# A fused attention and MLP kernel: MLP groups of 4, 6, 6, 6, 6, 4 and 4 chunks instead of nine groups of 4

## The chip, the cores and the metric

The kernel runs on one core of one Trainium2 chip. The metric is the device time of one execution in microseconds (us). Three runs of the kernel before took 2340.01, 2342.80 and 2343.21 us; their median, 2342.8 us, is the time before. TensorE is called PE here, its weight loads PEld, VectorE DVE, ScalarE ACT, GpSimd POOL, and SyncE, which issues nearly all transfers, SP.

## The reference

The input x is one sequence of 2048 tokens of width 576. Two branches read it, and a gate mixes them:

```python
x = A_x
g = _sigmoid((x * gate_w).sum(-1, keepdims=True))
a = _A_ref(x, A_wqkv, A_wo)     # 32-head attention, head width 18, softmax over 2048 keys
b = _B_ref(x, B_w1, B_b1, B_w2, B_b2)
return g * a + (1 - g) * b

def _B_ref(x, w1, b1, w2, b2):
    y = _layernorm(x, axis=-1)
    h = _gelu(jnp.einsum("bsd,df->bsf", y, w1) + b1)      # 576 -> 4608, tanh form of GELU
    return jnp.einsum("bsf,fd->bsd", h, w2) + b2          # 4608 -> 576
```

All data are 32-bit floats. Products are made from rounded high parts and their remainders (high x high, high x low, low x high), which is why each weight and activation appears as a pair of tiles.

## The kernel before, in words

**Three stretches.** First come the QKV projection, the layer norm and the gate (the first 250 us or so). Then a loop of 512 steps runs the attention, and the whole MLP is cut into pieces that are put between the attention's matmuls. The output projection begins in the last dozen steps and ends alone after the loop.

**The attention step.** There are 32 units (a pair of heads, half of the queries), and each has 16 steps, one per chunk of 128 keys. A step issues, twice: two score matmuls (line 248, called s2 here), whose results ACT turns into exponentials (line 251), and one round of two score matmuls for a later unit (line 208, called s1), whose maxima DVE takes (line 210). An even step also issues the products of probabilities and values for the last two steps (line 266). The s1 rounds run ahead of s2 and end some 20 steps before the loop does. At the end of a unit's rounds its maxima are transposed on PE (line 225) and written by two small transfers into the next query tile; these go out on ACT's queue instead of SP's where a large load of y was issued in the last 20 slots (lines 229 and 122). Five PSUM banks go round for the scores, and two (`ps_w`) belong to the MLP and later to the output projection.

**The pieces.** `mlp()` (line 319) is a generator that yields after every few matmuls. The loop calls `fill` three times in two steps: at the end of an even step (share 0) and twice in the odd step (shares 1 and 2). Each call takes one piece from the generator. A double step, counted from the start of an odd step to the start of the next odd one, thus holds eight s2 and eight s1 matmuls, one block of line 266 and three MLP pieces. Each engine's instructions stand in the order in which this Python code issues them; nothing is reordered later. A slot is one call of `run_due`; there are eight in a double step, and deferred work (GELU stages, weight splits, stores) is issued at slots or when a running estimate of POOL's queue falls due.

**The MLP.** Tokens go in four blocks of 512, the 4608 hidden units in 36 chunks of 128. `h_pair` (line 428) makes two chunks: 27 slots of two matmuls (line 452, 64 rows each, both halves of the array at once), 54 matmuls in all. DVE and ACT add the bias (lines 472 and 473), and GELU runs on ACT (square, line 505; tanh, line 503) and POOL (line 164), six POOL operations per chunk, ending in a high and a low tile (`hp` pool, 6 buffers of each). `out_pair` (line 510) multiplies one group of chunks into 128 tokens: 2 turns x G chunks x 3 products x 2 halves. The second turn swaps the PSUM banks of the two halves, so `nc.tensor.drain()` (line 521) stands between the turns. Then two DVE operations (line 541) add half of each bank's sum into `acc`. A group needs four `out_pair` calls.

With G = 4 there are nine groups in a block. The order (lines 597 to 611) is: first pair of group i, the four `out_pair` of group i-1, loads or splits of the down weights of group i, second pair of group i. The first pair of a group is called with `last=True` and is cut into six pieces of 8, 10, 10, 8, 10 and 8 matmuls (two double steps); the second is cut into three pieces of 18 (one double step). An `out_pair` is cut after 14 and 30 of its 48 matmuls and takes one double step. In a block's last group the second pair stands between the `out_pair` calls. In the first block every weight is read raw, rounded on ACT (line 368), split on POOL and stored to a scratch in DRAM; later blocks reload the pairs from it (W1 pairs 1152 KB, W2 chunks 576 KB; `wp2` has 4 buffers for W2).

**The end.** At steps 489, 494, 497 and 499 (`PSTEP`) the output projection's generator is advanced by hand: wo is loaded, then the attention output (line 915), then its denominators (line 934), and then five multiplications, roundings and differences on DVE and ACT (lines 978, 981 and 988, for the last chunk 984, 985 and 990) are issued slot by slot. Projection pieces of nine matmuls (line 1052) replace MLP pieces once the MLP generator is empty, all sums are stored (line 548), and the step is past 500. Until then an empty generator gives an empty piece.

Of the kernel before, what the change touches and what calls it, by code (L numbers as in the profile page):

```python
# [24 lines left out]
TB = 512  # L25
NPAIR = H // 2
VW = 52
G = 4
NFC = F // P
NG = NFC // G  # L30
ND = 288
SCALE = DH ** -0.5
GC1 = 0.7978845608028654 * 0.044715
# [7 lines left out]
LAND = 8  # L41
GAP = 1130.0
BUSY = 20
TOTAL = NB * NG * (G // 2 * 27 * 231 + 8 * 3 * G * 131)
PLAN = [[(), (0,), (1,), (2,), (3,), (4,), (5, 6), ()], [(), (), (0,), (1,), (2,), (3,), (4,), (5, 6)],
        [(0,), (1,), (2,), (3,), (4,), (5,), (6,), ()]]
LAST = 28
PSTEP = (489, 494, 497, 499)
ORDER = (0, 1, 3, 2)
ROUNDS = [lambda g: 0, lambda g: 0, lambda g: int(g >= 4), lambda g: 1 if g < 9 else 2]  # L50
SKIP = 0
N_AT = 5
# [6 lines left out]
def gated_mix_kernel(ctx: ExitStack, tc: tile.TileContext, x, wqkv, wo, w1, b1, w2, b2, gate_w, out):  # L59
# [24 lines left out]
    b2b = const.tile([P, D], F32, name="b2b")  # L84


    att = ctx.enter_context(tc.tile_pool(name="att", bufs=1))
    yp = ctx.enter_context(tc.tile_pool(name="yp", bufs=2))
    xp = ctx.enter_context(tc.tile_pool(name="xp", bufs=2))
    pp = ctx.enter_context(tc.tile_pool(name="pp", bufs=2))  # L90
    hp = ctx.enter_context(tc.tile_pool(name="hp", bufs=6))
    asm = ctx.enter_context(tc.tile_pool(name="asm", bufs=2))
    ps_s1 = ctx.enter_context(tc.tile_pool(name="ps_s1", bufs=NS1, space=PSUM))
    ps_o = ctx.enter_context(tc.tile_pool(name="ps_o", bufs=1, space=PSUM))
# [19 lines left out]
    def x_tile():  # L114
        return xp.tile([P, 4 * 640], F32, name="x")
# [203 lines left out]
    def mlp():  # L319
# [1 line left out]
        RAW = {}  # L321
        seq = [(tb, g) for tb in range(NB) for g in range(NG)]
        n = len(seq)
        npair = n * (G // 2)
        Y, ACC = {}, {}

        def chunk(q):

            i, m = divmod(q, G // 2)
            return i, m, seq[i][1] * G + 2 * m  # L330


        raws = x_tile()
# [67 lines left out]
                split(W1, q, wp1, shape, (1, q), R1, w1_scr[q], lambda q: load_w1(q + 1))  # L401

        def prep_w2(i):
            for m in range(G // 2):
                q = i * (G // 2) + m
                for j in range(2):
                    c = 2 * (q % NQ0) + j
                    if q >= NQ0:
                        reload(W2, (q, j), wp2, [P, 2, D], w2_scr[c])
                        continue  # L410
                    split(W2, (q, j), wp2, [P, 2, D], (2, c), R2[c % 2], w2_scr[c],
                          lambda c: load_w2(c + 2))
# [97 lines left out]
        def out_pair(i, t, acc):  # L510

            tb, g = seq[i]
            tok = slice(t * P, (t + 1) * P)
            cs = [slice(nn * ND, (nn + 1) * ND) for nn in range(2)]
            ps = [psum(ps_w) for _ in range(2)]
            ends = {7, 15} if piece[0] == 0 else cuts(24, (3, 2, 1)[piece[0]])
            k = 0
            for turn in range(2):
                if turn == 1:

                    nc.tensor.drain()
                for j in ORDER:
# [4 lines left out]
                    w_ = ready(W2, (i * (G // 2) + j // 2, j % 2))  # L527
                    for h_, p_ in ((hh, 0), (hh, 1), (hl, 0)):
                        for h in (0, 1) if turn == 0 else (1, 0):
                            r = slice(64 * h, 64 * h + 64)  # L530
                            nn = h ^ turn
                            nc.tensor.matmul(ps[nn][:, :ND], h_[r, tok], w_[p_][r, cs[nn]],  # L532
                                             start=(k == 0), stop=(k == 6 * G - 1))
                        k += 1
                        if k < 6 * G:
                            if k in ends:
                                cut[0] = 1
                            yield 131
            for nn in range(2):
                dst = acc[:, t, cs[nn]]  # L540
                nc.vector.scalar_tensor_tensor(dst, ps[nn][:, :ND], 0.5, b2b[:, cs[nn]] if g == 0 else dst,  # L541
                                               op0=ALU.mult, op1=ALU.add)
# [18 lines left out]
        def outs(i, between=()):  # L561

            tb, g = seq[i]
            if g == 0:
                ACC[tb] = x_tile().rearrange("p (t d) -> p t d", t=4)[:, :, :D]
# [4 lines left out]
            for j in range(G):  # L570
                HT.pop((i, j))
                W2.pop((i * (G // 2) + j // 2, j % 2))

        load_w1(0)
        for c in range(2):
# [10 lines left out]
        def pair(q, ahead, last=False, inner=False):  # L586
            prep(q + ahead)
            yield from h_pair(q, last, inner)
            i, m, _ = chunk(q)
            if m == 1 and seq[i][1] == NG - 1:  # L590
# [4 lines left out]


        for i in range(n + 1):
            q = 2 * i
            inside = i < n and seq[i][1] == NG - 1
            held = 1 if 0 < i < n and seq[i][1] == 0 else 2  # L600
            if i < n:
                yield from pair(q, held, last=i > 0)
                prep(q + 1 + held)
                if i == n - 1:
                    borrow_w2(q)
            if i > 0:
                yield from outs(i - 1, pair(q + 1, 2, inner=True) if inside else ())
            if 0 < i < n - 1:
                prep_w2(i)
            if i < n and not inside:  # L610
                yield from pair(q + 1, held)

    stream = [mlp()]
    spent = [0.0]
# [33 lines left out]
    with ExitStack() as a:  # L648
# [172 lines left out]
        for tb in range(NB):  # L821
            work = [(qk_group, (tb, mt)) for mt in (range(9) if tb < 2 else (4, 0, 1, 2, 3, 5, 6, 7, 8))] + [(v_group, (tb, t, n)) for t in range(4) for n in range(2)]
            for g, (fn, args) in enumerate(work):
                if tb == 0:
                    if g in W_AT:
                        n = W_AT[g]
                        split_w(n, nc.gpsimd if n > 1 else nc.vector)
                        if n + 2 < 6:
                            load_w(n + 2)
                    if g == 10:  # L830
                        nc.sync.dma_start(b2b, bcast_rows(b2, D))
                        nc.sync.dma_start(b1r, b1.rearrange("(c p) -> c p", p=P))
                if tb == NB - 1 and g == 16:
                    args += (lambda: next(stream[0]),)
                fn(*args)
                ng = g - (N_AT if tb == 0 else 2)
                if 0 <= ng < 4:
                    norm(tb, ng)
                if tb + 1 < NB and 2 <= g < 7:
                    x_chunk(tb + 1, g - 2)  # L840
                yg = g - (11 if tb == 0 else 8)
                if 0 <= yg < 5:
                    y_chunk(tb, yg)
                if g == (16 if tb == 0 else 13) and tb + 2 < NB:
# [311 lines left out]
```

## Time and profile before

| | before |
|---|---|
| median of three runs | 2342.8 us |
| the profiled execution, its own time | 2341.28 us |
| its span in the trace | 2339.5 us |
| PE busy | 2297.5 us (98%) |
| DVE busy | 1655.2 us (71%) |
| ACT busy | 1424.9 us (61%) |
| POOL busy | 966.3 us (41%) |
| mean granted PE clock | 0.994 |

The span is the stretch from the first to the last instruction; the time of an execution is 1.8 us longer. A row of grouped instructions gives line, engine, operation, tiles, shapes, count, then busy time, mean ns of one, then idle time before them and what ended it. A row of the timeline gives start, duration, engine, line and, in brackets, the idle time before it with its releaser. A row of a table by stretches gives the stretch's bounds and length, the busy time of each engine with its instruction count, then the granted clock, the share of the transfer engines and GB/s. Matmuls are pipelined: their durations overlap, so the distance from one start to the next is the better measure of what one costs.

### The profile page before, as it was taken

How to read it: one execution, taken by the hardware profiler on the slowest of the kernel's cores; microseconds unless marked ns; L12 is line 12 of the kernel's file. 1: busy time of each engine (PE TensorE's matmuls, PEld its weight loads, DVE VectorE, ACT ScalarE, POOL GpSimd, SP SyncE). 2: the span in 40 equal slices, each digit the busy share in tenths (PEclk: the TensorE clock that was granted, in tenths of full speed). 3: DMA queues.
4: the chain of work that ended last, by engine and by line, in shares of the span. 5: the costliest groups of instructions: out<-in, count | busy, mean ns of one | idle time of the engine just before them, and what ended most of it. 6: DMA issues, size and time to landing. Idle time of an engine off the chain costs nothing.

```text
span 2339.5 us, 51512 instructions
## 1 busy us (share of the span) xinstructions
PE 2297.5 (98%) x20585; PEld 1571.1 (67%) x20585; DVE 1655.2 (71%) x2890; ACT 1424.9 (61%) x2628; POOL 966.3 (41%) x964
## 2 busy tenths in 40 slices
PE   8999999999999999999999999999999999999999
PEld 7876666666666666666666666666666666666668
DVE  5466677777777777777777777777777777777734
ACT  4222467777676666666666666666666666666662
POOL 3001366666664433333352444444434333333700
PEclk9999899999999999999999999999999999999999
DMA  7648754545456423243263524242364233242264
GB/s 233 237 177 231 198 184 128 169 130 153 136 188 166 158 95 118 93 120 122 82 167 135 163 95 118 95 138 96 118 160 151 95 103 105 101 146 88 80 212 160
DMA packets 164010, 330.31 MB, mean 141 GB/s; under 512 B 57034, under 2 KB 83694, under 8 KB 153042
## 3 DMA queue, kind: packets, MB, share of 16 engines
q1 hardware_dynamic: 162150, 323.76, 44.2%
q8 instruction: 162, 2.65, 0.5%
q10 hardware_dynamic: 1620, 3.26, 0.4%
q14 instruction: 78, 0.64, 0.1%
HBM read 234.16 MB, written 96.58 MB: 141 GB/s over the span
## 4 chain that ended last, share of the span: by engine, by line
PE 94%; DVE 3%; issue 1%; DMA 1%; ACT 1%; SPq 0%; ACTq 0%; DVEq 0%
PE ps L532 21%; PE ps L266 20%; PE ps L452 19%; PE ps L248 13%; PE ps L208 11%; PE ps L769 4%; PE ps L1052 3%; PE ps L790 2%; DVE m L210 1%; PE ps L696 1%; DMA vt<-v_scr 1%; DVE p L756 0%; PE ps L772 0%; PE ps L771 0%; DMA p<-in_A_wqkv_dram 0%
## 5 line engine op out<-in xcount | busy, mean ns | idle before, releaser
L210 DVE TENSOR_REDUCE m<-ps 128x1 f32<-128x512 f32 x2048 | 1316.5, 685 | 465.0 <-PE ps L208 448.1
L251 ACT ACTIVATE p<-ps 128x512 f32<-128x512 f32 x1368 | 742.4, 596 | 408.7 <-PE ps L248 399.3
L164 POOL TENSOR_SCALAR zz<-zz 128x512 f32<-128x512 f32 x288 | 178.4, 620 | 832.0 <-ACT zz L505 816.6
L452 PE MATMUL ps<-big,w 64*128 64x512 f32 x3888 | 513.3, 393 | 0.1
L532 PE MATMUL ps<-w,hh 64*128 64x288 f32 x4352 | 490.7, 299 | 12.2 <-ACT z L473 0.4
L251 ACT ACTIVATE ring<-ps 128x512 f32<-128x512 f32 x680 | 369.3, 596 | 204.8 <-PE ps L248 200.5
L208 PE MATMUL ps<-ka,qa 54*128 54x512 f32 x2048 | 456.0, 415 | 12.1 <-DVE m L210 5.0
L248 PE MATMUL ps<-qa,ka 56*128 56x512 f32 x2048 | 453.8, 423 | 1.2 <-ACT p L251 1.0
L452 PEld LDWEIGHTS ps<-big,w 64*128 64x128 f32 x3888 | 380.7, 185 | 75.3 <-ACT z L473 0.4
L532 PEld LDWEIGHTS ps<-w,hh 64*128 64x128 f32 x4352 | 383.5, 186 | 68.6 <-issue 45.1
L164 POOL TENSOR_TENSOR zz<-zz,z 128x512 f32<-128x512 f32 x288 | 371.7, 1291 | 24.0
L248 PEld LDWEIGHTS ps<-qa,ka 56*128 56x128 f32 x2048 | 205.2, 184 | 214.8 <-DVE m L210 178.8
L266 PE MATMUL ps<-p,vt 128*32 128x512 f32 x2736 | 344.8, 598 | 1.2 <-DMA vt<-v_scr 1.2
L532 PE MATMUL ps<-w,hl 64*128 64x288 f32 x2176 | 334.5, 292 | 0.0
L208 PEld LDWEIGHTS ps<-ka,qa 54*128 54x128 f32 x2048 | 213.7, 187 | 84.4 <-ACT p L251 25.3
L164 POOL TENSOR_TENSOR w<-x,w 128x576 fp32r<-128x576 f32 (+1 forms) x54 | 98.5, 1838 | 307.6 <-DMA qk_scr<-hl 169.0
L532 PEld LDWEIGHTS ps<-w,hl 64*128 64x128 f32 x2176 | 218.1, 185 | 4.9
L164 POOL TENSOR_TENSOR hl<-zz,hh 128x512 fp32r<-128x512 f32 x136 | 176.6, 1298 | 11.4
L266 PEld LDWEIGHTS ps<-p,vt 128*32 128x32 f32 x2736 | 71.6, 109 | 160.8 <-issue 151.8
L266 PE MATMUL ps<-ring,vt 128*32 128x512 f32 x1360 | 179.1, 598 | 0.0
L769 PE MATMUL ps<-big,wqk 128*128 128x512 f32 x432 | 110.6, 405 | 2.9 <-ACT wqk L690 2.0
L541 DVE SCALAR_TENSOR_TENSOR x<-ps,x 128x288 f32<-128x288 f32 x256 | 104.1, 448 | 12.7 <-PE ps L532 12.7
(100 smaller groups left out, 1375.3 us busy)
## 6 DMA issues: line engine op xcount, KB each, us to landing
w<-w_scr SPq DMA_DIRECT2D x54, 1152.0 KB
w<-w_scr SPq DMA_DIRECT2D x108, 576.0 KB
x<-in_B_w_dram SPq DMA_DIRECT2D x72, 288.0 KB
w_scr<-w SPq DMA_DIRECT2D x18, 1152.0 KB
w_scr<-w SPq DMA_DIRECT2D x36, 576.0 KB
big<-y_scr SPq DMA_DIRECT2D x42, 384.0 KB
qa<-qk_scr SPq DMA_DIRECT2D x192, 72.0 KB
ka<-qk_scr SPq DMA_DIRECT2D x84, 144.0 KB
```

The source lines that it names most:

```text
L164: fn(*args, **kw)
L208: nc.tensor.matmul(ps, qa[r0:r0 + 54, t * P:(t + 1) * P], ka[r0:r0 + 54, kb * TB:(kb + 1) * TB], start=True, stop=True)
L210: nc.vector.tensor_reduce(M4[u][:, h, t, kb:kb + 1], ps, axis=AX.X, op=ALU.max)
L248: nc.tensor.matmul(ps[h], ka[r0:r0 + 56, kc * P:(kc + 1) * P], qa[r0:r0 + 56, qb * TB:(qb + 1) * TB], start=True, stop=True)
L251: nc.scalar.activation(RING[n % 3][:, qb, h], ps[h], AF.Exp, scale=SCALE)
L266: nc.tensor.matmul(OB[u][r:r + 32, :], v[:, k, 19 * h:19 * h + 32], RING[c % 3][:, qb, h, :], start=(k == 0), stop=(k == NT - 1))
L452: nc.tensor.matmul(ps[h], wt[w_][r, c, :], Y[s_][r, c, :], start=(k == 0), stop=(k == 26))
L532: nc.tensor.matmul(ps[nn][:, :ND], h_[r, tok], w_[p_][r, cs[nn]], start=(k == 0), stop=(k == 6 * G - 1))
L541: nc.vector.scalar_tensor_tensor(dst, ps[nn][:, :ND], 0.5, b2b[:, cs[nn]] if g == 0 else dst, op0=ALU.mult, op1=ALU.add)
L769: nc.tensor.matmul(ps, w_[:, c, ms], big[:, s_, :], start=(k == 0), stop=False)
L790: nc.tensor.matmul(ps[:, :ND], big[:, s_, tok], w_[:, c, cs], start=(k == 0), stop=False)
L1052: nc.tensor.matmul(ps[:, :ND], OT[b][2][:, s_, tok], w_part(w_, c)[:, cs], start=(k == 0), stop=(k == 13))
```

## The change

The groups of a block become 4, 6, 6, 6, 6, 4 and 4 chunks. There are 28 groups instead of 36, and 112 `out_pair` calls instead of 144, with as many matmuls as before. For the larger groups `hp` has 8 buffers of each kind, and `wp2` has 6. An `out_pair` of six chunks has 72 matmuls, cut into three pieces of 24, with the drain in the middle of the second. All pairs of a group after the first are issued one behind the other, and every pair but those between the `out_pair` calls and the first two is called with `last=True`, so that it takes six pieces (one pair, which the code finds late, five). The bias b2 is no longer held in a tile and added at the first sum: `begin_sums` loads it, broadcast, into `acc` by four transfers of 288 KB on SP per block, one up pair ahead of the block's first sum. The order of the chunks in a sum is 0 to n-3, then n-1, n-2 (for four chunks the same as before). The space for the tiles comes from a smaller reserve (`dynamic_dma_scratch_size`). In the instruction order of the changed program the last MLP matmul stands in step 495 instead of 499; the `PSTEP` numbers and the step from which the projection may begin are the same.

```diff
-G = 4
 NFC = F // P
-NG = NFC // G
+SIZES = (4, 6, 6, 6, 6, 4, 4)
+NG = len(SIZES)
...
-TOTAL = NB * NG * (G // 2 * 27 * 231 + 8 * 3 * G * 131)
+TOTAL = NB * (NFC // 2 * 27 * 231 + 8 * 3 * NFC * 131)
...
-ORDER = (0, 1, 3, 2)
...
-    hp = ctx.enter_context(tc.tile_pool(name="hp", bufs=6))
+    hp = ctx.enter_context(tc.tile_pool(name="hp", bufs=8))
...
+        size = [SIZES[g] for _, g in seq]
+        npair = NB * NFC // 2
...
+        place = [(i, m) for i in range(n) for m in range(size[i] // 2)]
+        first_pair = [place.index((i, 0)) for i in range(n)]
...
         def prep_w2(i):
-            for m in range(G // 2):
-                q = i * (G // 2) + m
+            for m in range(size[i] // 2):
+                q = first_pair[i] + m
...
-            ends = {7, 15} if piece[0] == 0 else cuts(24, (3, 2, 1)[piece[0]])
+            half = 3 * size[i]
+            ends = {7, 15} if piece[0] == 0 and half == 12 else cuts(2 * half, (3, 2, 1)[piece[0]])
+            order = [*range(size[i] - 2), size[i] - 1, size[i] - 2]
...
-                nc.vector.scalar_tensor_tensor(dst, ps[nn][:, :ND], 0.5, b2b[:, cs[nn]] if g == 0 else dst,
+                nc.vector.scalar_tensor_tensor(dst, ps[nn][:, :ND], 0.5, dst,
                                                op0=ALU.mult, op1=ALU.add)
...
+        def begin_sums(tb):
+
+            ACC[tb] = x_tile().rearrange("p (t d) -> p t d", t=4)[:, :, :D]
+            for t in range(4):
+                nc.sync.dma_start(ACC[tb][:, t], bcast_rows(b2, D))
...
         for i in range(n + 1):
-            q = 2 * i
+            q = first_pair[i] if i < n else npair
             inside = i < n and seq[i][1] == NG - 1
             held = 1 if 0 < i < n and seq[i][1] == 0 else 2
+            if i > 0 and seq[i - 1][1] == 0:
+                begin_sums(seq[i - 1][0])
...
             if i < n and not inside:
-                yield from pair(q + 1, held)
+                for m in range(1, size[i] // 2):
+                    yield from pair(q + m, held, last=i > 0)
...
-                        nc.sync.dma_start(b2b, bcast_rows(b2, D))
                         nc.sync.dma_start(b1r, b1.rearrange("(c p) -> c p", p=P))
...
-                        wp2 = mstack.enter_context(tc.tile_pool(name="m_w2", bufs=4))
+                        wp2 = mstack.enter_context(tc.tile_pool(name="m_w2", bufs=6))
...
-    nc = _bacc.Bacc("TRN2", target_bir_lowering=False, num_devices=1)
+    nc = _bacc.Bacc("TRN2", target_bir_lowering=False, num_devices=1, dynamic_dma_scratch_size=1024)
```

More of the change, by code (lines that the diff above doesn't have):

```diff
@@ L83, in gated_mix_kernel @@
     b1t = const.tile([P, NFC], F32, name="b1t")
-    b2b = const.tile([P, D], F32, name="b2b")
     att = ctx.enter_context(tc.tile_pool(name="att", bufs=1))
@@ L323, in mlp @@
         n = len(seq)
-        npair = n * (G // 2)
+        size = [SIZES[g] for _, g in seq]
+        npair = NB * NFC // 2
         Y, ACC = {}, {}
+        place = [(i, m) for i in range(n) for m in range(size[i] // 2)]
+        first_pair = [place.index((i, 0)) for i in range(n)]
         def chunk(q):
-            i, m = divmod(q, G // 2)
-            return i, m, seq[i][1] * G + 2 * m
+            i, m = place[q]
+            return i, m, 2 * (q % (NFC // 2))
         raws = x_tile()
@@ L521, in out_pair @@
                     nc.tensor.drain()
-                for j in ORDER:
+                for j in order:
                     while (i, j) not in HT:
@@ L526, in out_pair @@
                     hh, hl = HT[i, j]
-                    w_ = ready(W2, (i * (G // 2) + j // 2, j % 2))
+                    w_ = ready(W2, (first_pair[i] + j // 2, j % 2))
                     for h_, p_ in ((hh, 0), (hh, 1), (hl, 0)):
@@ L532, in out_pair @@
                             nc.tensor.matmul(ps[nn][:, :ND], h_[r, tok], w_[p_][r, cs[nn]],
-                                             start=(k == 0), stop=(k == 6 * G - 1))
+                                             start=(k == 0), stop=(k == 2 * half - 1))
                         k += 1
-                        if k < 6 * G:
+                        if k < 2 * half:
                             if k in ends:
@@ L563, in outs @@
             tb, g = seq[i]
-            if g == 0:
-                ACC[tb] = x_tile().rearrange("p (t d) -> p t d", t=4)[:, :, :D]
             for t in range(4):
@@ L569, in outs @@
                 yield from out_pair(i, t, ACC[tb])
-            for j in range(G):
+            for j in range(size[i]):
                 HT.pop((i, j))
-                W2.pop((i * (G // 2) + j // 2, j % 2))
+                W2.pop((first_pair[i] + j // 2, j % 2))
+        def begin_sums(tb):
+            ACC[tb] = x_tile().rearrange("p (t d) -> p t d", t=4)[:, :, :D]
+            for t in range(4):
+                nc.sync.dma_start(ACC[tb][:, t], bcast_rows(b2, D))
         load_w1(0)
@@ L589, in pair @@
             i, m, _ = chunk(q)
-            if m == 1 and seq[i][1] == NG - 1:
+            if m == size[i] // 2 - 1 and seq[i][1] == NG - 1:
                 hidden[0] = seq[i][0]
```

## The prediction

> **What bounds the kernel now.** I read the page first, then the chain of waits, then the loop by double steps.
>
> ```profile
> span 2339.5 us, 51512 instructions
> PE 2297.5 (98%) x20585; PEld 1571.1 (67%) x20585; DVE 1655.2 (71%) x2890; ACT 1424.9 (61%) x2628; POOL 966.3 (41%) x964
> PE 94%; DVE 3%; issue 1%; DMA 1%; ACT 1%; SPq 0%; ACTq 0%; DVEq 0%
> PE ps L532 21%; PE ps L266 20%; PE ps L452 19%; PE ps L248 13%; PE ps L208 11%; PE ps L769 4%; PE ps L1052 3%; PE ps L790 2%; DVE m L210 1%; PE ps L696 1%; DMA vt<-v_scr 1%; DVE p L756 0%; PE ps L772 0%; PE ps L771 0%; DMA p<-in_A_wqkv_dram 0%
> ```
>
> The chain of work that ended last is PE for 94%. A busy share alone would not show that PE is full, since matmuls overlap; starts do. The timeline prices one piece of 18 up matmuls and one `out_pair` around its drain:
>
> ```profile
> 999.08 2.26 PE L452 MATMUL ps<-big,w 64*128 64x512 f32 x18
> 1001.17 0.40 PE L248 MATMUL ps<-qa,ka 56*128 56x512 f32 x2
> ```
> ```profile
> 1135.46 0.30 PE L532 MATMUL ps<-w,hh 64*128 64x288 f32 x2
> 1135.59 0.30 PE L532 MATMUL ps<-w,hl 64*128 64x288 f32 x2
> 1135.73 0.42 PE L532 MATMUL ps<-w,hh 64*128 64x288 f32 x4
> 1135.99 0.30 PE L532 MATMUL ps<-w,hl 64*128 64x288 f32 x2
> 1136.37 0.53 PE L532 MATMUL ps<-w,hh 64*128 64x288 f32 x4
> 1136.74 0.30 PE L532 MATMUL ps<-w,hl 64*128 64x288 f32 x2
> 1136.87 0.41 PE L248 MATMUL ps<-qa,ka 56*128 56x512 f32 x2
> ```
> ```profile
> PEld ps L532 <- issue: 45.1, 144, 0.5
> ```
>
> An up matmul costs (1001.17 - 999.08)/18 = 0.116 us, a pair of down matmuls 0.13 us. From 1135.99 to 1136.37, over the drain, it is 0.38 instead of 0.13, and the next two pairs take 0.37 instead of 0.26: a drain costs 0.36 us. The waits show 144 such holes of 45.1/144 = 0.31 us on the weight side; I take 0.35. Now double steps, in a table by stretches:
>
> ```profile
> 340.58:348.60 8.02, 8.00 (x63) 4.58 (x60) 5.16 (x9) 6.31 (x13) 7.68 (x8) 1.00 0.37 99
> 676.91:684.91 8.00, 7.99 (x62) 4.63 (x60) 5.16 (x9) 6.30 (x13) 7.66 (x8) 1.00 0.91 339
> 740.97:748.51 7.54, 7.54 (x66) 4.56 (x64) 5.75 (x10) 6.93 (x14) 4.39 (x4) 1.00 0.62 236
> 781.57:790.61 9.04, 9.04 (x78) 6.07 (x76) 5.25 (x9) 5.82 (x11) 1.30 (x2) 1.00 0.87 299
> 790.61:797.84 7.23, 7.23 (x62) 4.40 (x60) 5.17 (x9) 5.39 (x11) 6.80 (x8) 1.00 0.49 146
> 797.84:804.93 7.09, 7.09 (x67) 4.39 (x64) 5.89 (x11) 5.96 (x12) 4.69 (x6) 1.00 0.89 154
> 804.93:812.44 7.51, 7.43 (x84) 5.08 (x82) 5.79 (x11) 5.37 (x11) 7.00 (x9) 1.00 1.01 392
> ```
>
> By the order of the matmuls, the fourth row has 44 up matmuls, the fifth 28, the sixth 18 up and 14 down, the seventh 48 down and a drain. Taking off 44 x 0.116 and 28 x 0.116 leaves 3.94 and 3.98 for the attention part; I use 3.94. Then the seventh row, 3.94 + 24 x 0.133 + 0.35 = 7.48, holds 0.03 us of waiting, the fifth 0.03, the sixth (3.94 + 2.09 + 0.93 = 6.96) 0.13. PE has next to no idle time to give away here: a removed drain is a gain, and anything that makes PE wait is a loss.
>
> **The change part by part.**
>
> *Drains.* 112 instead of 144: -32 x 0.35 = -11.2 us (bounds 0.31 and 0.38: -9.9 to -12.2). All other matmuls of PE remain.
>
> *Evictions and b2.*
>
> ```profile
> L541 DVE SCALAR_TENSOR_TENSOR x<-ps,x 128x288 f32<-128x288 f32 x256 | 104.1, 448 | 12.7 <-PE ps L532 12.7
> ```
>
> DVE loses 64 x 0.448 = 28.7 us, but waits for PE in each double step (5.79 of 7.51 busy): nothing on the path. The b2 loads add 15 transfers of 288 KB to SP's queue, four at a time, one up pair (14 us, fifth and sixth row) ahead of their use; the seventh row moved 392 GB/s, so 1.2 MB are 3 us. Six W2 reloads (3.5 MB, 9 us at that rate) stand at least two up pairs ahead of use. SP waits there for the last matmul of `outs`, as before; the query and key loads behind it are for a later unit. Both 0. Without that cover DVE's sums would wait first, then `ps_w`, then PE.
>
> *Up pairs over two double steps, blocks 1 to 3.* A pair in one double step waits for nothing (fourth row: what is left there is the base of 3.94), one in two costs 0.03 + 0.13 = 0.16 us: GELU then shares ACT and DVE with scores that come faster. 51 pairs instead of 27 are so cut: +3.8. Of down double steps there are 84 instead of 108, and the longer pieces give ACT and DVE more time: I take off 2 of the 108 x 0.03 = 3.2 that they held. Together +1.8 (0 to +4).
>
> *The same in block 0.* Here ACT also rounds weights.
>
> ```profile
> L251 ACT ACTIVATE p<-ps 128x512 f32<-128x512 f32 x1368 | 742.4, 596 | 408.7 <-PE ps L248 399.3 <-PE ps L208 2.6 <-PE ps L532 0.9
> L505 ACT ACTIVATE zz<-z 128x512 f32<-128x512 f32 x144 | 83.5, 639 | 1.4 <-DVE z L472 1.2
> L368 ACT ACTIVATE w<-x 128x576 fp32r<-128x576 f32 (+1 forms) x54 | 43.6, 845 | 2.3 <-DMA x<-in_B_w_dram 2.2
> ```
>
> Eight exponentials are 4.8 us; two tanh or squares and two rounded W2 chunks bring ACT to some 7.3 us in a double step of 28 up matmuls that PE could do in 7.2. That is the first row (8.02, so 0.8 of waiting); seven such stand in block 0, the second row is the last. By the instruction order each of the four groups of six has three crowded double steps: two W2 roundings beside bias and squares (the third row of the table: 7.54 against 6.97, 0.57), two beside the tanh (0.8), one W1 rounding beside bias and squares (7.9 us of ACT in 7.64, 0.3). 4 x 1.7 = 6.8, plus two of 0.57 in the groups of four, against 7 x 0.8 = 5.6 and one 0.57: +1.8, and I add 1 for a unit's end that now falls into a short double step. +2.8. The low bound is 0; at the high one each of a group's six double steps of up pairs waits 0.8 like the first row: 4 x 4.8 + 1.1 - 6.2 + 1 = +15.
>
> *Rows on ACT's queue.* Two units' rows instead of one follow a load of y within 20 slots.
>
> ```profile
> 1710.89 1.91 ACTq L122 DMA_DIRECT2D qa<-mr  x2
> 1712.85 1.08 ACT L251 ACTIVATE p<-ps 128x512 f32<-128x512 f32 x2 [1.98 <-PE ps L248]
> 1713.49 0.99 PE L208 MATMUL ps<-ka,qa 54*128 54x512 f32 x2 [1.07 <-ACT p L251]
> ```
> ```profile
> 1712.14:1715.55 3.41, 2.26 (x18) 1.45 (x18) 1.61 (x3) 2.58 (x5) 2.07 (x4) 1.00 1.06 220
> 1715.55:1718.96 3.41, 3.41 (x30) 3.25 (x28) 1.29 (x2) 1.60 (x3) 3.16 (x4) 0.50 0.84 172
> ```
>
> ACT stood 1.91 us for two issues, PE waited about 1.7, and then the granted clock was 0.50 for 3.41 us, another 1.7. In the changed order the y loads stand over 10 us ahead of the rows, so I take 1.1 us for each and a half clock in one case of three: 2 x (1.1 + 0.6) - 3.4 = 0 (-1 to +3.4).
>
> *The end.* The MLP is done four steps earlier, and the projection starts no earlier.
>
> ```profile
> 2228.93:2235.47 6.54, 6.46 (x77) 4.42 (x74) 1.51 (x3) 4.34 (x9) 0.74 (x1) 1.00 0.06 21
> 2235.47:2241.99 6.52, 6.44 (x76) 4.39 (x74) 1.08 (x3) 4.34 (x9) 0.74 (x1) 1.00 0.65 207
> 2241.99:2247.87 5.88, 5.80 (x63) 3.70 (x59) 4.30 (x8) 5.08 (x10) 0.00 (x0) 1.00 0.55 176
> ```
> ```profile
> 2237.92 0.39 SPq L934 DMA_DIRECT2D ka<-ot_scr  x1
> 2243.57 1.90 DVE L978 TENSOR_TENSOR x<-x,ka 128x512 f32<-128x512 f32 x3 [4.00 <-DMA ka<-ot_scr]
> 2244.30 1.24 ACT L981 ACTIVATE big<-x 128x512 fp32r<-128x512 f32 x2 [0.73 <-DVE x L978]
> 2263.58 0.69 DVE L978 TENSOR_TENSOR x<-x,den 128x512 f32<-128x512 f32 x1 [5.94 <-DMA den<-ot_scr]
> 2265.52 0.50 PE L248 MATMUL ps<-qa,ka 56*128 56x512 f32 x1 [1.02 <-ACT p L251]
> ```
>
> These are the double steps of steps 495, 497 and 499, 18.94 us. Without 48 + 48 of their down matmuls and two drains PE would need 18.94 - 7.1 = 11.8. But the denominators, issued 2.45 us into step 497 and landed 5.65 us later, hold DVE, ACT's roundings behind it and the exponentials behind those. After: 497 begins at 5.6 (the 5.88 row less its wait), the issue at 7.6 (one store less ahead of it), landing at 13.3; from there DVE's first operation (0.7), three roundings (1.24 for two, so 1.9) and four exponentials (2.1) stand before the banks of step 501's scores are free: 18.0. So 18.0 against 11.8 is +6.2; the next denominators (last rows) are no longer behind late stores and PE's wait of 1.02 there goes: -1. +5.2 (+2.5, with ACT alone as the limit, 8 x 0.55 per double step, to +8).
>
> Sum against the profiled execution, 2341.28: -11.2 + 1.8 + 2.8 + 0 + 5.2 = -1.4, so 2339.9. The median of the runs is 1.5 us above that execution: 2341.4.
>
> **The rivals.** (1) The saving arrives nearly whole. For it: a wait in block 0 needs ACT's crowding to add up, and in the first row ACT is busy for only 6.31 of 8.02; if it adds nothing and the end costs 2.5, the sum is -11.2 + 1.8 + 2.5 = -6.9: 2335.9.
>
> (2) On the other side: ACT falls behind in block 0 and stays behind. Three pairs follow each other, in the first row POOL is busy for 7.68 of 8.02 us, and a tanh that waits for POOL holds all exponentials behind it. At the high bound, +15 instead of +2.8, the sum is +10.8: 2353.6. It decides (0.2% slower than the median) from 1.7 + 6.1/4 = 3.2 us of waiting per group of six. Against it: the same engines have the whole down part of a group to catch up.
>
> (3) The half clock. In the row above it followed a stretch in which PE idled for about a third of 3.41 us; the empty steps leave PE without work for some 6 us in all. Two half-clock windows, 1.7 each, and one more after ACT's queue: +5.1, so 2346.5. The Trainium skill, "TensorE: Matmul & The Clock Gate", Part 1, says that the clock halves after an idle window of about 3.4 us and returns after a busy one. The trace does not agree with the first half: PE worked for 2.26 of the 3.41 us ahead of the drop. By the page's rule the end would cost at most one such window, 1.7.
>
> (4) The drains cost nothing, because DVE and ACT catch up in them. Then all that is left is +9.8: 2352. The seventh row speaks against it: its length is the sum of its parts.
>
> **How the numbers follow.** A measurement of this kernel can tell about 0.2% (4.7 us, so 2338.1 to 2347.5) from no change. The forecast, no change, has 0.41; (1) has 0.27 and is faster; (2) 0.19, (3) 0.08, (4) 0.05. (2) and (4) are slower; (3) lies near the edge and is shared, 0.04 and 0.04. So faster 0.27, same 0.45, slower 0.28. The forecast's own range is 2338 to 2347. The range for 8 in 10 goes from 2334 (rival 1 with the drain at its upper bound and less than 0.16 per up pair) to 2350 (rival 2 at 3.8 us per group of six); the rest of (2), (4) and a tail below are left out.
>
> **What would show it.** 112 holes before line 535 with the same mean; double steps of 72 down matmuls and a drain of 3.94 + 4.79 + 0.35 = 9.1 us; block 0 (steps 13 to 121) with about 3 us more waiting; a double step of steps 497 and 499 that is not 3.0 us but 4 to 7, with DVE waiting for `ka`. I am wrong if a wait appears that no row above has: sums waiting for b2, or scores waiting for the rows behind six W2 loads.

## The result and the profile after

The changed kernel takes 2355.5 us (median of four runs, 2354.04 to 2356.19), the kernel before 2341.9 beside it: a ratio of 1.0057, 95% interval 1.0041 to 1.0073. It is slower by 0.57% and lies above the predicted range of 2334 to 2350. The profiled execution took 2356.05 us.

The page of the changed kernel: its span, the busy times, and the chain of work that ended last, by engine and by line.

```profile
span 2354.3 us, 51380 instructions
...
PE 2300.6 (98%) x20585; PEld 1565.5 (66%) x20585; DVE 1635.6 (69%) x2826; ACT 1423.6 (60%) x2628; POOL 965.1 (41%) x964
...
PE 87%; POOL 4%; DVE 3%; issue 2%; DMA 2%; ACT 1%; SPq 1%; ACTq 0%; POOLq 0%; DVEq 0%
```

PE still reads as 98% busy. The chain tells that the waits have changed: PE's share fell from 94% to 87%, and POOL, which was not in it, has 4%. These shares are no price: 4% of the span would be 94 us, and a kernel below (`both_moved`) has POOL at 5% and takes 17 us less. Two groups of ACT's instructions show new waits, one of them for POOL. Each row ends with ACT's idle time ahead of the group and what ended it; first the kernel before (tanh, weight rounding), then the changed one.

```profile
L503 ACT ACTIVATE zz<-zz 128x512 f32<-128x512 f32 x144 | 91.3, 634 | 0.0
L368 ACT ACTIVATE w<-x 128x576 fp32r<-128x576 f32 (+1 forms) x54 | 43.6, 845 | 2.3 <-DMA x<-in_B_w_dram 2.2
```
```profile
L504 ACT ACTIVATE zz<-zz 128x512 f32<-128x512 f32 x144 | 91.2, 633 | 12.9 <-POOL zz L162 12.9
L369 ACT ACTIVATE w<-x 128x576 fp32r<-128x576 f32 (+1 forms) x54 | 43.8, 844 | 12.2 <-DMA x<-in_B_w_dram 12.0
```

ACT now waits 12.9 us for POOL ahead of the tanh and 12 us for raw weight loads ahead of roundings, with exponentials queued behind both. To see what PE pays, I take each double step's length and subtract its parts: as in the prediction 3.94 for the attention (3.0 once the s1 rounds are over), 0.0667 per down matmul and 0.35 per drain; 0.1165 per up matmul, where the prediction had 0.116; and, read from starts in the same traces, 0.133 per projection matmul and 0.24 for a transpose of maxima. What is left I call its waiting.

| steps | waiting before, us | after | difference | predicted |
|---|---|---|---|---|
| 13 to 122 (block 0) | 11.9 | 29.6 | +17.7 | +2.8 |
| 123 to 490 | 18.7 | 18.4 | -0.3 | +1.8 and 0 |
| 491 to 500 | 0.3 | 10.1 | +9.8 | the end, |
| 501 to 510 | 7.9 | 6.2 | -1.7 | +5.2 in all |
| 32 drains x 0.35 | | | -11.2 | -11.2 |

The sum is +14.3 of the 14.8 us by which the spans of the two profiled executions differ. A table of the changed kernel by stretches (bounds, length, busy time of PE, PEld, DVE, ACT, POOL with counts, granted clock, share of the transfer engines, GB/s) shows the double steps that matter:

```profile
345.82:353.82 8.00, 7.97 (x63) 4.58 (x60) 5.31 (x10) 6.30 (x13) 7.34 (x8) 1.00 0.66 225
376.26:386.32 10.06, 9.88 (x108) 6.98 (x106) 5.98 (x10) 5.61 (x11) 9.47 (x10) 1.00 0.57 177
672.00:689.29 17.29, 10.12 (x61) 5.00 (x58) 5.82 (x10) 7.16 (x14) 6.50 (x6) 0.70 0.95 257
1482.84:1491.91 9.07, 8.99 (x109) 6.72 (x106) 6.52 (x11) 4.34 (x8) 0.00 (x0) 1.00 0.01 2
2247.89:2252.56 4.67, 4.39 (x26) 1.65 (x24) 0.83 (x2) 4.03 (x8) 0.00 (x0) 1.00 0.33 96
2252.56:2263.96 11.40, 6.80 (x28) 1.90 (x24) 5.36 (x9) 6.70 (x14) 0.00 (x0) 0.90 0.63 201
```

The fourth row is a double step of 72 down matmuls in a later block, 9.07 us as predicted; the second is one in block 0, 10.06. The third is step 99: 17.29 us for work of 6.97. The last two are the double steps 497 and 499, which hold no MLP matmul. Here is step 99, on SP's queue, ACT and PE:

```profile
665.94 2.06 SPq L120 DMA_DIRECT2D qa<-qk_scr  x6
668.05 2.12 SPq L120 DMA_DIRECT2D ka<-qk_scr  x6
670.27 0.39 SPq L192 DMA_DIRECT2D vt<-v_scr  x1
670.75 7.61 SPq L354 DMA_DIRECT2D x<-in_B_w_dram  x2
```
```profile
672.50 1.09 ACT L249 ACTIVATE p<-ps 128x512 f32<-128x512 f32 x2 [0.32 <-PE ps L246]
680.31 0.68 ACT L369 ACTIVATE w<-x 128x576 fp32r<-128x576 f32 x1 [6.72 <-DMA x<-in_B_w_dram]
...
682.09 1.06 ACT L249 ACTIVATE p<-ps 128x512 f32<-128x512 f32 x2
```
```profile
675.15 0.40 PE L246 MATMUL ps<-qa,ka 56*128 56x512 f32 x1
682.72 0.79 PE L246 MATMUL ps<-qa,ka 56*128 56x512 f32 x1 [7.17 <-ACT p L249]
```

In the second step of every other unit SP issues the queries, keys and values of a coming pair of heads. Behind them a raw load of two W2 chunks needs 7.61 us to go out; this I call a meeting of loads. ACT's rounding of these chunks is already in its queue and waits 6.72 us; the exponentials behind it keep the PSUM banks of the scores; PE stands for 7.17 us and then needs 0.79 us for what took 0.40. The granted clock is 0.50 from 677.9 to 688.1 us; PE works for 5.4 us of that, which costs it about 2.7 us more. Of block 0's 17.7 us, this one meeting is 10.

### The profile page after: what moved, and what is told of

It reads as the page before. It is cut to its first block, busy times and chain, and to the rows that moved or that the text cites. A ratio compares the mean times of both kernels' runs of the same rounds, so it can differ in the third digit from the quotient of the medians.

```text
span 2354.3 us, 51380 instructions
## 1 busy us (share of the span) xinstructions
PE 2300.6 (98%) x20585; PEld 1565.5 (66%) x20585; DVE 1635.6 (69%) x2826; ACT 1423.6 (60%) x2628; POOL 965.1 (41%) x964
## 4 chain that ended last, share of the span: by engine, by line
PE 87%; POOL 4%; DVE 3%; issue 2%; DMA 2%; ACT 1%; SPq 1%; ACTq 0%; POOLq 0%; DVEq 0%
PE ps L535 20%; PE ps L264 19%; PE ps L453 17%; PE ps L246 12%; PE ps L206 10%; PE ps L779 4%; PE ps L1061 3%; POOL zz L162 2%; PE ps L800 2%; DVE m L208 1%; POOL w L162 1%; DMA x<-in_B_w_dram 1%; POOL hl L162 1%; DMA vt<-v_scr 1%; PE ps L706 1%
## 5 line engine op out<-in xcount | busy, mean ns | idle before, releaser
L453 PE MATMUL ps<-big,w 64*128 64x512 f32 x3888 | 528.4, 393 | 0.9 <-ACT z L474 0.8
L535 PE MATMUL ps<-w,hh 64*128 64x288 f32 x4352 | 467.2, 297 | 9.5
L246 PE MATMUL ps<-qa,ka 56*128 56x512 f32 x2048 | 458.7, 424 | 11.5 <-ACT p L249 10.2
L535 PEld LDWEIGHTS ps<-w,hh 64*128 64x128 f32 x4352 | 376.6, 185 | 57.5 <-issue 35.3
L162 POOL TENSOR_TENSOR hl<-zz,hh 128x512 fp32r<-128x512 f32 x136 | 176.7, 1300 | 11.4
L544 DVE SCALAR_TENSOR_TENSOR x<-ps,x 128x288 f32<-128x288 f32 x224 | 91.6, 450 | 26.8 <-PE ps L535 26.8
```

Of the source, the lines that this page charges most:

```text
L162: fn(*args, **kw)
L246: nc.tensor.matmul(ps[h], ka[r0:r0 + 56, kc * P:(kc + 1) * P], qa[r0:r0 + 56, qb * TB:(qb + 1) * TB], start=True, stop=True)
L453: nc.tensor.matmul(ps[h], wt[w_][r, c, :], Y[s_][r, c, :], start=(k == 0), stop=(k == 26))
L544: nc.vector.scalar_tensor_tensor(dst, ps[nn][:, :ND], 0.5, dst, op0=ALU.mult, op1=ALU.add)
```

## The experiments

Ratios are to the kernel before on the same chip (2340.7 to 2340.9 us), where the changed kernel, which was not run again beside them, would be at about 2354 by its ratio.

**The price of a drain.** `drain_twice`:

```diff
                 for j in order:
+                    if turn == 1 and j == order[size[i] // 2]: nc.tensor.drain()
```

> The changed kernel with one more drain in the middle of the second turn of each out_pair, 112 in all. If a drain costs PE what the rows gave (0.35 us): +39 us, 2395. If DVE and ACT catch up in drains and they cost nothing (rival 4): 0 to +5, up to 2360.

2389.2 us, ratio 1.0207 (1.0188 to 1.0226): 35 us more than the changed kernel, 0.31 us for each of the 112 (0.26 to 0.37 by the two intervals). The waits show the holes on the weight side doubled, first the changed kernel, then `drain_twice`:

```profile
PEld ps L535 <- issue: 35.3, 112, 0.5
```
```profile
PEld ps L536 <- issue: 70.7, 224, 0.5
```

The 0.31 us are a net price. The 29 double steps of 72 down matmuls in blocks 1 to 3 that have no transpose went from a median of 9.07 to 9.42 us, 0.35 for the drain; in return the waiting of steps 13 to 122 is 3.3 us less than in the changed kernel, and that of steps 491 to 500 2.7 us less. So a drain costs PE time, and rival 4 is out.

**Block 0 alone undone.** `block0_fours`:

```diff
+BLOCKS = ((4,) * 9, SIZES, SIZES, SIZES)
-                    yield from pair(q + m, held, last=i > 0)
+                    yield from pair(q + m, held, last=seq[i][0] > 0)
```

> The changed kernel with nine groups of four in the first block, their second pairs in one double step as before, and 4, 6, 6, 6, 6, 4, 4 in the other three; the last MLP matmul stays in step 495. Theory Q+C: all that block 0 lost (waiting of 29.6 us against 11.9) is the larger groups' doing, so -17.7, and 8 drains more, +2.8: 2340.6 us. If only the meeting of the value load with a raw W2 load mattered and the groups of four meet it too, only the crowding goes: -7.6 + 2.8, 2350.7. If block 0 has nothing to do with it, +2.8: 2358.

2343.5 us, ratio 1.0013 (1.0004 to 1.0021). Block 0's waiting is 12.2 us, step 99's 0.2. Nearly the whole loss of block 0 belongs to the larger groups there. The run does not tell the meeting of loads from crowding, that is, from more work on ACT and POOL than a double step has room for.

**The meeting of loads.** `v_parts` cuts the value load into four:

```diff
...
-                    load_v(u // 2 + 1)
+            if kc in (1, 3, 5, 7) and u % 2 == 0 and u // 2 + 1 < NPAIR: load_v(u // 2 + 1, 2 * kc - 2, 2 * kc + 2)
```

> The changed kernel with the value load of the next pair of heads (416 KB in rows of 208 bytes, one transfer) cut into four of 104 KB, two steps apart. Theory Q (queue): in step 99 a raw load of W2 stood 7.61 us in SP's queue behind that load, ACT's rounding of it waited 6.72 us with all exponentials behind, PE stood 7.17 us, and then ran at half clock (10.3 us in all); steps 39 and 43 lost 3.9 us by the same meeting at step 33. Then 10 to 13 us go: 2342.5 to 2345.5 us. Theory C (crowding): three up pairs in a row in block 0 keep ACT and POOL late, whatever the loads do; then at most 2 us go: 2353.5 to 2356. In both the end (steps 497 to 501, 16.1 us) stays.

2351.8 us, ratio 1.0049 (1.0037 to 1.0062), about 2 us gained and not 10. Step 39 lost its 2.0 us, step 99 went from 10.3 to 8.4 only. The rows of this run say why:

```profile
668.80 0.39 SPq L192 DMA_DIRECT2D vt<-v_scr  x1
669.28 1.37 SPq L354 DMA_DIRECT2D x<-in_B_w_dram  x2
...
677.04 1.40 ACT L369 ACTIVATE w<-x 128x576 fp32r<-128x576 f32 x2 [5.30 <-DMA x<-in_B_w_dram]
```

The raw load now goes out in 1.37 us, but lands 6 to 8 us later, behind the queries and keys: the value load is not the whole obstacle. `loads_late` moves all three loads three double steps later in block 0:

```diff
-            if kc == 1:
+            if kc == (7 if u < 8 else 1):
                 if u + 2 < NU:
                     load_q(u + 2)
```

> The changed kernel with the query, key and value loads of the next pair of heads three double steps later in the first block (at the eighth step of a unit instead of the second), so that the raw loads of W2 in steps 33 to 38 and 97 to 101 have no such loads ahead of them. The run with the value load in four parts took only 2 us of the 10.3 out of step 99: there the raw W2 load went out 1.5 us sooner, but it still stood behind 0.9 MB of query and key loads and landed 7.7 us later. Theory Q2 (it is all of the loads at a pair's change, in issue and in bytes, that make the raw load late): the whole of step 99's stall and the 2.0 us of step 39 go, -11 to -13: 2341.5 to 2343.5 us where the changed kernel would be at 2354. Theory R (the raw load is late because of POOL's split and the scratch store on which SP waits 11.6 us ahead of it, loads or no loads): the stall stays, 0 to -3.

2351.0 us, ratio 1.0045 (1.0033 to 1.0058): another miss in the total, and the most telling run. Step 99's waiting fell from 10.3 to 0.6, and step 41's rose from 0.8 to 10.0. There the moved loads met the raw load of another group:

```profile
424.68 0.39 SPq L192 DMA_DIRECT2D vt<-v_scr  x1
425.37 8.00 SPq L354 DMA_DIRECT2D x<-in_B_w_dram  x2
...
435.57 0.68 ACT L369 ACTIVATE w<-x 128x576 fp32r<-128x576 f32 x1 [6.84 <-DMA x<-in_B_w_dram]
```

The stall goes where the meeting goes. `loads_moved` puts them where there is none: unit 6 alone gets its loads three double steps later, and for unit 2 alone the value load goes out in four parts.

```diff
...
-            if kc == 1:
+            if kc == (7 if u == 6 else 1):
...
-                    load_v(u // 2 + 1)
+                    if u != 2: load_v(u // 2 + 1)
+            if u == 2 and kc in (1, 3, 5, 7): load_v(u // 2 + 1, 2 * kc - 2, 2 * kc + 2)
```

> The changed kernel with the query, key and value loads of unit 6 alone three double steps later (step 103 instead of 97), and the value load of unit 2 in four parts two steps apart. In the run with all such loads later in block 0, step 99 fell from 10.3 to 0.6 us of waiting, but step 41 rose from 0.8 to 10.0: the loads at step 39 now met the raw W2 load there. If the place where a pair's loads meet a raw W2 load is all that matters, both steps stay clean here and steps 39 to 43 too: -11.7, 2342 us where the changed kernel would be at 2354. If something else makes the raw load late in this part of block 0, a stall of 7 to 10 us comes up at another step: 2350 or more.

2344.4 us, ratio 1.0013 (1.0004 to 1.0021): 10 us gained. Block 0's waiting is 18.0 us, and ACT's wait ahead of roundings is back where it was before the change:

```profile
L369 ACT ACTIVATE w<-x 128x576 fp32r<-128x576 f32 (+1 forms) x54 | 43.6, 845 | 2.7 <-DMA x<-in_B_w_dram 2.7
```

**The end.** First the rows of the changed kernel: the denominators' issue, DVE's first use, and ACT behind it.

```profile
2251.28 0.39 SPq L943 DMA_DIRECT2D ka<-ot_scr  x1
...
2258.60 1.90 DVE L987 TENSOR_TENSOR x<-x,ka 128x512 f32<-128x512 f32 x3 [7.91 <-DMA ka<-ot_scr]
2259.33 1.23 ACT L990 ACTIVATE big<-x 128x512 fp32r<-128x512 f32 x2 [4.45 <-DVE x L987]
2261.10 1.48 PE L264 MATMUL ps<-p,vt 128*32 128x512 f32 x3 [4.32 <-ACT p L249]
```

`end_spread` puts MLP matmuls into steps 497 and 499 again, by cutting the last down matmuls finer:

```diff
+            ends = cuts(2 * half, (6, 5, 4)[piece[0]]) if i == n - 1 and t in (2, 3) else ...
```

> The changed kernel with the last two out_pair calls cut into six pieces instead of three, so that the last MLP matmul stands in step 499 again and steps 497 and 499 are not empty; PE's work is the same. Theory E (empty steps): the denominators' landing and the roundings behind it hold PE for 10.0 us in steps 497 and 499 because nothing else is there; with MLP pieces there the waiting falls to that of before (0.2), and steps 501 to 511 go back from 6.2 to 7.9 us of waiting: -8, 2347.5 us. Rival: the landing is late by itself and holds the exponentials, so PE stalls in these steps with or without pieces: 0 to -3, 2352.5 to 2355.5.

2351.9 us, ratio 1.0049 (1.0036 to 1.0063), some 2 us gained, as the rival said. Step 499 still waits 7.2 us although it now holds 16 down matmuls: the denominators land no sooner. `end_early` issues them sooner, in two parts and into a place that is free sooner, and starts the projection sooner:

```diff
-PSTEP = (489, 494, 497, 499)
+PSTEP = (485, 490, 492, 495)
...
+            if b == 0:
+                wide = [wp2.tile([P, 2, D], F32R, name="w3")... for _ in range(2)]
```

> The changed kernel with the output projection's preparation at steps 485, 490, 492 and 495 instead of 489, 494, 497 and 499, its first denominators in two free W2 buffers instead of the key tile of unit 30 (free only from step 496 on), and the first projection matmul in step 497 instead of 501. The spread end showed that the landing of the denominators holds DVE, ACT and PE for 7 us whether steps 497 and 499 have MLP matmuls or not. Theory D (it is this transfer, issued behind the stores at the unit's end): with it issued 20 us sooner nothing stands in 497 to 501, and these steps take 54 projection matmuls off the part behind the loop: -7 to -9, 2345 to 2347 us where the changed kernel would be at 2354. Rival: the wait moves to the next block's denominators, whose unit is done four steps too late for it: -2 to 0.

2360.4 us, ratio 1.0086 (1.0074 to 1.0099): a loss. The 8.4 us in step 499 are 1.7, but the 54 projection matmuls that moved into steps 497 and 499 bring nothing: from step 511 to the last matmul it takes 47.2 us with them done, 46.8 without. Step 501 waits 2.1 us more. (The profiled execution, 2357.2 us, is the fastest of five, and its span is only 1.1 us longer than the changed kernel's; what the slower ones lost besides is in no trace.) Behind the loop, DVE and PE stand for the last unit's denominators:

```profile
2317.89 0.69 DVE L994 TENSOR_TENSOR x<-x,qa 128x512 f32<-128x512 f32 x1 [5.04 <-DMA qa<-dn_scr]
...
2319.24 0.85 PE L1068 MATMUL ps<-big 128*128 128x288 f32 x2 [5.02 <-DVE big L1004]
```

Projection work that is left over the loop's end covers that landing; done sooner, it only lengthened the loop. `den_early_spread` keeps the projection at step 501, and takes the early denominators (`PSTEP = (489, 491, 493, 499)`) and the finer cuts:

> The changed kernel with the first denominators in two W2 buffers at step 493 (as in the run that prepared the projection early), but the projection from step 501 as in the changed kernel, and the last two out_pair calls cut into six pieces, so that steps 491 to 499 have 16 to 24 down matmuls each and their attention is bound by ACT's eight exponentials (4.7 us). In the run prepared early the wait in 499 was gone, but the projection then ran out of work: behind the loop PE stood 5.0 us for the last unit's denominators, which come about 15 us after the loop whatever was done before. Theory: with the wait removed and the projection not begun sooner, 491 to 501 lose 9 to 10 us of waiting and the part behind the loop gets at most 2 us longer: -7 to -8, 2346 to 2347 us where the changed kernel would be at 2354. Rival: the time behind the loop grows by as much as the loop shrinks: 0 to -3.

2347.7 us, ratio 1.0026 (1.0017 to 1.0036): 7 us gained. Steps 491 to 500 wait 1.2 us instead of 10.1, steps 501 to 510 some 2 us more, and the part behind the loop is 46.8 us again. The landing, not the emptiness by itself, was the loss, together with ACT's eight exponentials, which hold a double step at 4.67 us (step 497) where PE alone would need 3.0.

**The tanh behind POOL.** `tanh_late`:

```diff
-                    queue_end(200.0, lambda: second(w, parts))
+                    queue_end(2800.0 if tb == 0 else 200.0, lambda: second(w, parts))
```

> The changed kernel with the tanh of the first block issued 2.6 us (of the running estimate of POOL's queue) later. In the four double steps of 72 down matmuls of block 0 (steps 29, 49, 69 and 89) the tanh waits for POOL, which has a split of 2.66 us ahead of the GELU, and ACT stands up to 2.64 us with exponentials behind it: 0.97 + 1.17 + 1.20 + 1.18 = 4.5 us of PE waiting. If that is rival 2's mechanism in small: -3 to -4.5 us, 2349.5 to 2351 where the changed kernel would be at 2354. If the crowding only moves to the next double steps: -1 to +2. The stall of step 99 and the end stay in both.

2372.8 us, ratio 1.0134 (1.0118 to 1.0149): far off both expectations. ACT's wait for POOL ahead of the tanh did go:

```profile
L504 ACT ACTIVATE zz<-zz 128x512 f32<-128x512 f32 x144 | 90.6, 634 | 0.6 <-POOL zz L162 0.6
```

but the order of everything behind a late tanh changed: 14.6 us came up in steps 1 to 12, and steps 29, 49, 69 and 89 wait 2.0 us each instead of 1.1. In step 3 ACT now stood 9.55 us ahead of a W1 rounding (at 285.20). The profile names no releaser for it, but the times do: the raw load of these weights went out right behind a value load (273.59), from 274.08 on, and by the trace's semaphore events its last part landed at 285.13. It is the meeting of loads once more. In the changed kernel the same load lands at 286.5 and no engine waits, since other work stands ahead of the rounding on ACT until 288.41. A delay put into an in-order stream moves more than the one instruction.

`all_three` joins `loads_late`, `end_early` and `tanh_late`:

> Loads of a pair of heads later in block 0, projection prepared earlier, and tanh later in block 0, all in the changed kernel. If the three causes are separate, their gains add: -11 - 8 - 4 = -23, so 2331 us where the changed kernel would be at 2354, and below the kernel before by 10. If the raw loads stay late whatever stands ahead of them, 2341; if the three are one and the same slack, 2343.

2375.4 us, ratio 1.0147 (1.0133 to 1.0161): far from all three expectations and as bad as the worst of its parts; it tells nothing that they do not.

**Both real causes removed.** `both_moved` is `loads_moved` with the end of `den_early_spread`:

> The loads of loads_moved and the end of den_early_spread in one kernel. If block 0's stall and the end are separate losses of the larger groups, this is -11.7 - 7.5 = -19: 2335 us where the changed kernel would be at 2354 and the kernel before at 2341; what is left of the 32 drains is then a gain of 0.25%.

2336.8 us, ratio 0.9985 (0.9976 to 0.9994): about 17 us below the changed kernel, the sum of the two gains, and below the kernel before. `fours_end` is `block0_fours` with that end:

> Groups of four in block 0 (as in block0_fours, which took 2343.5 us) and the end of den_early_spread: 2343.5 - 7.5 = 2336 us. Against both_moved it tells what groups of six are worth in block 0: 8 drains (2.8 us) against the crowding there (7.6 us, of which 2 are gone with the loads moved); by that, both are within 2 to 3 us of each other.

2335.5 us, ratio 0.9977 (0.9968 to 0.9986), the fastest here. Against `both_moved` it is 1.4 us, less than the intervals can part. By the waits, the groups of six cost 6.1 us more in steps 13 to 122; eight drains fewer are worth 2.8, and steps 123 to 490 wait 3.0 us less behind them. The chain of `fours_end` is that of the kernel before again:

```profile
PE 93%; DVE 3%; DMA 2%; issue 1%; ACT 1%; SPq 0%; ACTq 0%; POOL 0%; DVEq 0%
```

**What crowds block 0.** `w1_on_dve` is `both_moved` with the low part of a W1 split on DVE, `fours_w1_on_dve` the same on `fours_end`:

```diff
-                pool_op(src.free_size(), nc.gpsimd.tensor_tensor, t[:, 1], src, t[:, 0].bitcast(F32), op=ALU.subtract)
+                nc.vector.tensor_tensor(t[:, 1], src, t[:, 0].bitcast(F32), op=ALU.subtract) if raw[0] == 1 and looped[0] else pool_op(...)
```

> both_moved with the low part of a W1 split made on DVE instead of POOL (18 operations of 2.66 us leave POOL). Still open is why block 0 keeps 18 us of waiting against 11.9 with groups of four, although its stalls behind loads are gone. Theory P: in steps 29, 49, 69 and 89 a W1 split stands on POOL ahead of the GELU, the tanh waits for it, and the exponentials behind the tanh: 4.6 us, which go: 2332 us where both_moved has 2336.8. Theory A (ACT itself is full there with W1 roundings, tanh and exponentials, POOL only comes last): 0 to -1. Rival: the subtraction holds DVE, which then takes the maxima later, and PE waits for PSUM banks: slower by up to 4.

> The control: fours_end with the low part of a W1 split on DVE. With groups of four the double steps of 48 down matmuls in block 0 wait for nothing (none above 0.25 us but those with a transpose), so theory P and theory A both say no change, 2335.5 within 1 us; if DVE is held by the subtraction, slower by up to 4.

2342.6 us, ratio 1.0007 (0.9998 to 1.0017), and 2346.7 us, ratio 1.0027 (1.0017 to 1.0037): 6 us lost against `both_moved` and 11 against `fours_end`. In step 69 of `w1_on_dve`, DVE waits for ACT's rounding, subtracts, and the maxima pile up behind:

```profile
548.68 1.70 DVE L373 TENSOR_TENSOR w<-x,w 128x1152 fp32r<-128x1152 f32 x1 [1.63 <-ACT w L369]
550.30 2.47 DVE L208 TENSOR_REDUCE m<-ps 128x1 f32<-128x512 f32 x4
551.03 0.49 PE L206 MATMUL ps<-ka,qa 54*128 54x512 f32 x1 [0.87 <-DVE m L208]
```

where the same step of `both_moved` has ACT's tanh behind POOL's split of 2.66 us:

```profile
544.49 2.66 POOL L162 TENSOR_TENSOR w<-x,w 128x1152 fp32r<-128x1152 f32 x1 [3.65 <-ACT w L369]
...
549.25 0.63 ACT L504 ACTIVATE zz<-zz 128x512 f32<-128x512 f32 x1 [2.65 <-POOL zz L162]
...
550.42 0.50 PE L246 MATMUL ps<-qa,ka 56*128 56x512 f32 x1 [0.24 <-ACT p L249]
```

The wait for POOL is gone and the one for DVE dearer: the rival of the expectation. That POOL's split holds the tanh is in the rows; that the 4.6 us would come back without it is not shown, since neither run took it away without a new wait.

## Why the prediction was wrong, point by point

*Drains: right.* 112 holes of 35.3/112 = 0.315 us, as before the change (0.313). Within a double step a drain costs the 0.35 taken; the net price by the doubled drains is 0.31, the lower bound.

*Evictions and b2: right.* No sum waits for b2, and steps 123 to 490 have no stall that the loads of W2 explain.

*Up pairs over two double steps, blocks 1 to 3: near the low bound.* Predicted +1.8 (0 to +4); the waiting of steps 123 to 490, with the rows on ACT's queue in it, moved by -0.3. Without step 123, in which the kernel before waits 1.5 us and the changed one 0.2, it is +1.0.

*Rows on ACT's queue: right.* 0 predicted; steps 235, 237 and 365 wait 0.8 + 1.1 + 1.25 = 3.2 us, where step 365 waited 3.4 before. No half clock followed.

*The same in block 0: the step that failed.* It said +2.8, with a high bound of +15, and +17.7 came. The meetings of loads are 11.6 of it, down double steps behind POOL's splits 4.5, and the rest 1.6. Three parts:

- The prediction costed roundings by ACT's busy time alone and gave no term to the wait of a rounding for its raw load, though its own row of the roundings (line 368) has that wait, as 2.2 us; it became 12.0. The change moves the raw loads in SP's queue against the loads of a pair of heads. A meeting stood in the trace of before, and did no harm there, since ACT had no rounding to do until 424.05:

```profile
402.93 7.05 SPq L353 DMA_DIRECT2D x<-in_B_w_dram  x2
```

  That is 10.3 us in step 99 and 2 in step 39, of which `loads_moved` took back 10 in time and 11.6 in block 0's waiting. The prediction followed SP's queue for b2 and for the W2 reloads, and ACT's for the rows, but not SP's for the raw loads of block 0.
- The up part was priced well: 1.7 per group of six predicted; the three crowded double steps of the first such group wait 0.57 + 0.58 + 0.80 = 1.95 (step 21 is the first row of the table by stretches).
- The prediction took the down double steps in block 0 as free of waiting, from a row without GELU's tanh behind a W1 split. Steps 29, 49, 69 and 89 wait 0.97 + 1.17 + 1.20 + 1.18 = 4.5 us. That POOL's split is the cause is read from the rows; no run shows it by taking it away.

*The end: right in its mechanism, short in size.* Predicted from the start of 495 to step 501: 18.0 us; measured 5.59 + 4.67 + 11.40 = 21.66. The issue of the denominators came at 9.0 us instead of 7.6, and the landing took 7.3 us instead of 5.65. The second double step took 11.4 us, where the prediction's last list had 4 to 7. The further -1 predicted was -1.7. So +8.1 instead of +5.2, at the upper bound of +8. With this term as predicted the time would have been some 2352.6, still above the range.

*The rivals.* Rival 2's time (2353.6) was the nearest to the result, but by luck. Its mechanism, ACT late in block 0, is there: a group of six waits 1.95 us in its crowded up double steps and 1.1 behind POOL in a down one, some 3.1 together, about the 3.2 at which the rival would begin to decide. But its high bound had 4.8 in the up double steps alone, and the larger loss came by a way that no rival had. Rival 3's half clock did come, in step 99 (mean 0.70) and in step 499 (0.90), each after a stand of PE and not by itself. The Trainium skill, "TensorE: Matmul & The Clock Gate", Part 1, has the clock halve after an idle window of about 3.4 us. The trace agrees only in part: PE stood longer than that in step 99, but the clock fell at 677.9, 2.4 us after PE's last matmul, and the 3.41 us ahead of the drop held 1.06 us of work (0.59 us ahead of the drop in step 499). Rival 1 and the forecast had the drains' gain right and the rest too small.

## What to carry to other kernels

Where an in-order engine has an instruction that waits for a load, do not count only the work between issue and use: look at what stands ahead of that load in its queue, at every place where two periods (here groups of chunks and pairs of heads) can meet, and look again when a change alters one period. A stall that disappears at one step should be looked for at others before the cause is called removed. At the end of this loop, work taken off PE was worth only what the latency behind it let through, and work moved ahead of a landing that came later anyway was worth nothing.

## What the hardware showed that was not expected

The next issue on the same queue behind a transfer of 416 KB in rows of 208 bytes took 5.6 to 8.4 us in the kernels before and after, but 2.2 us behind the changed kernel's last one. (The rows above, 7.05 and 7.61, and 8.00 in `loads_late`, are for two instructions.) With the transfer in four parts (`v_parts`), single issues behind a part took 0.3 to 1.3 us, and once 3.0. This occurs in the kernel before as well and was hidden there. And the time from step 511 to the last matmul was 46.8 us in all the kernels whose projection began in step 501, however the loop before it went.
